# Retention of eight heads beside an MLP on one core: chunk by chunk and placed late, instead of head pair by head pair

## The chip, the cores and the metric

The kernel runs on one core of one Trainium2 chip. The metric is the device time of one execution in microseconds (us), so lower is better. The engines are named as in the profile: PE is TensorE, PEld its weight load, DVE is VectorE, ACT is ScalarE, POOL is GpSimd, and SP is the engine that issues the input loads. "L282" is a line of the kernel that ran. An execution takes about 1.7 us longer than the span of its profile (387.5 against 385.8 for the kernel before).

## The reference

Eight sequences of 576 tokens pass through retention with eight heads of 64. The 4608 token vectors of 512 then pass through an MLP with a hard-swish.

```python
def _attn_ref(q, k, v):                       # each (8, 8, 576, 64)
    scores = np.matmul(q, k.transpose(0, 1, 3, 2)) / np.sqrt(64)
    gamma = 1.0 - 2.0 ** (-5.0 - np.arange(8))
    rel = np.arange(576)[:, None] - np.arange(576)[None, :]
    Dmat = np.where(rel >= 0, gamma[:, None, None] ** rel, 0.0)
    return np.matmul(scores * Dmat, v)

def _moe_ref(x, w_in, w_out):                 # (4608, 512), (512, 2048), (2048, 512)
    h = x @ w_in
    return (h * np.clip(h + 3.0, 0.0, 6.0) / 6.0) @ w_out
```

Because the decay is a power of the distance, retention can be done in chunks of 128 tokens. Inside a chunk it is masked scores times v. Across chunks it is q times a state, which is decayed by `gamma ** 128` a chunk and to which the sum of k times v of the chunk is added. A sequence is four full chunks and a remainder of 64 tokens.

## The kernel before

The kernel takes one **head pair** at a time, over all four full chunks of a batch (a batch is one sequence). `trans` brings k and q to the layout that the scores need, `score` makes scores and states, and `mix` makes the outputs. All PSUM tiles, into which PE's results go, come from one pool of eight, which rotates. [...] marks cuts.

```python
psum = ctx.enter_context(tc.tile_pool(name="psum", bufs=8, space=bass.MemoryType.PSUM))
[...]
def trans(b, pr):
    pst = psum.tile([P, 2 * NCH * P], FP16, tag="pp")
    [... eight transposes: k of chunks 0..3, then q of chunks 0..3 ...]
    t = work.tile([P, 2, NCH, P], FP16, tag="qkt", bufs=3)
    nc.vector.tensor_copy(t[:, 0]..., pst[:, 0:w])        # the k half, on VectorE
    nc.scalar.copy(t[:, 1]..., pst[:, w:2 * w])           # the q half, on ScalarE

def score(b, pr):
    [... scores of two heads into pms[0], pms[1]; k-v products of four chunks into pu ...]
    for h2 in range(2):
        nc.vector.tensor_tensor(out=at, in0=pms[h2], in1=cmask..., op=ALU.mult)
    nc.vector.tensor_copy(ss[:, 0, :], pu[:, 0, :])
    for c in range(1, NCH):                               # the state, chunk after chunk
        nc.vector.scalar_tensor_tensor(
            out=ss[:, c, :], in0=ss[:, c - 1, :], scalar=gch[:, pr:pr + 1],
            in1=pu[:, c, :], op0=ALU.mult, op1=ALU.add)
[...]
def groups(b):
    return [[(trans, 0)],
            [(score, 0), (trans, 1)],
            [(mix, 0), (score, 1), (trans, 2)],
            [(mix, 1), (score, 2), (trans, 3)],
            [(mix, 2), (score, 3), (trans_rem,)],
            [(mix, 3), (score_rem,)],
            [(mix_rem,)]]
```

The MLP runs in nine blocks of 512 tokens. A block has 32 sub-units of four matmuls each: 16 `up` and then 16 `down`. An `up` is followed by a relu on ScalarE and by a multiply on VectorE that needs it. A `down` leaves these two engines nearly free. The groups of the next batch stand at fixed places between sub-units:

```python
def up(kb, fc):
    [... four matmuls into ph ...]
    nc.scalar.activation(u, ph, ACTF.Relu, bias=cb[:, 0:1], scale=1.0 / 6.0)
    nc.vector.scalar_tensor_tensor(out=gts[kb][:, fc, :], in0=u, scalar=1.0,
                                   in1=ph, op0=ALU.min, op1=ALU.mult)
[...]
for g in groups(0):
    run(0, g)                                  # batch 0 wholly ahead of the MLP
for c in range(NCH + 1):
    load(1, c)
    scale(1, c)
for kb in range(NMB):
    gs = groups(kb + 1) if kb + 1 < B else []
    at_sub = {3 + 4 * i: g for i, g in enumerate(gs)}     # sub-units 3, 7, 11, ... 27
    for s in range(NSUB):
        up(kb, s) if s < NFC else down(kb, ...)
        if s in at_sub:
            run(kb + 1, at_sub[s])
        [... every sixth sub-unit: load and scale a chunk of batch kb + 2 ...]
```

`load` brings a chunk of k, q or v (256 KB in rows of 256 bytes). `scale` multiplies it with its decay weights and casts it, on GpSimd. The MLP's weights are fetched by requests in GpSimd's queue.

## Time and profile before

| | before |
|---|---|
| time, median of 4 executions | 386.61 us (386.09 to 387.2) |
| first MLP matmul | 35.58 us |
| first block of the MLP with batch 1 of retention | 58.91 us |
| each of the six next blocks with a batch of retention | 38.60 us |
| each of the two last blocks, no retention | 27.63 us |
| tail after the last block | about 4.2 us |

35.6 + 58.9 + 6 x 38.60 + 2 x 27.63 + 4.2 is the span, to 0.2 us. A block that holds a batch of retention costs 10.97 us more than one that doesn't, and the first block costs another 20.3 us.

First the page of the kernel before: busy time by engine, then the rows of the span in 40 equal slices (each digit is tenths of busy time; PEclk is the granted clock), then the chain of waits.

```profile
PE 331.4 (86%) x2560; PEld 166.9 (43%) x2560; DVE 195.5 (51%) x411; ACT 156.8 (41%) x277; POOL 101.5 (26%) x130
...
PE   0278219899989998999899989998999899999995
...
PEclk9999857999999999999999999999999999999999
DMA  9999999334924492349234923491440001002002
...
PE 65%; DVE 15%; DMA 8%; ACT 4%; issue 3%; POOL 2%; ACTq 0%; SPq 0%; POOLq 0%
```

No engine is full apart from PE. Yet the chain passes through DVE, ACT and DMA for 27% of the span. The PE row shows two places to look at: slices 5 and 6 (from 38.6 us), where PE is almost empty, and the regular "8" in every fourth slice after that.

**The empty stretch.** This is PE's timeline: start in us, length in us, line, operation, operands, count, and in brackets how long PE stood idle before it and what ended that.

```profile
35.58 5.01 PE L282 MATMUL ph<-xt_155,win_153 128*128 128x512 f16 x16
40.43 0.22 PE L153 MATMUL pst<-ident_90,natk_0_463 128*128 128x128 f16 x1
45.57 0.29 PE L153 MATMUL pst<-ident_90,natk_1_475 128*128 128x128 f16 x1 [4.92 <-POOL natk_1_475 L89]
52.84 0.29 PE L153 MATMUL pst<-ident_90,natk_2_487 128*128 128x128 f16 x1 [6.99 <-POOL natk_2_487 L89]
56.19 0.29 PE L153 MATMUL pst<-ident_90,natk_3_499 128*128 128x128 f16 x1 [3.06 <-POOL natk_3_499 L89]
```

After four sub-units (16 matmuls) PE meets the first transposes of batch 1. One group transposes all four chunks, so it waits until the last chunk has been loaded and scaled. PE works through its instructions in order, and the MLP behind it waits too. The loads are late because the weights arrive at the same time. This is the timeline of the queue that issues q, k and v (how long one request of 256 KB occupied the queue):

```profile
9.73 1.25 SPq L61 DMA_DIRECT2D stgk_3_84<-in_k_dram  x1
...
18.66 0.53 SPq L61 DMA_DIRECT2D stgq_0_459<-in_q_dram  x1
...
26.79 6.91 SPq L61 DMA_DIRECT2D stgq_1_471<-in_q_dram  x1
```

A request takes 0.5 to 1.3 us while q, k and v are alone, and 6 to 7 us while the weights come in.

**The regular gaps.** In the up half of a block, VectorE repeats this (its timeline, same columns):

```profile
107.73 2.48 DVE L288 SCALAR_TENSOR_TENSOR gt_1_1048<-u,ph 128x512 f16<-128x512 f32 x4 [1.24 <-ACT u L286]
110.13 0.68 DVE L180 TENSOR_TENSOR at<-pm_1233,cmask 128x512 f16<-128x512 f32 x1
110.73 0.68 DVE L180 TENSOR_TENSOR at<-pm_1234,cmask 128x512 f16<-128x512 f32 x1
111.33 0.28 DVE L187 CAST ss<-pu 128x128 f16<-128x128 f32 x1
111.64 1.11 DVE L189 SCALAR_TENSOR_TENSOR ss<-ss,gch,pu 128x128 f16<-128x128 f16 x3
112.67 0.42 DVE L158 COPY t<-pst 128x512 f16<-128x512 f16 x1
114.33 2.48 DVE L288 SCALAR_TENSOR_TENSOR gt_1_1048<-u,ph 128x512 f16<-128x512 f32 x4 [1.24 <-ACT u L286]
```

And ScalarE does this at the same time:

```profile
113.12 0.58 ACT L160 COPY t<-pst 128x512 f16<-128x512 f16 x1 [3.21 <-DVE t L158]
113.61 2.43 ACT L286 ACTIVATE u<-ph,cb 128x512 f32<-128x512 f32 x4
```

A group takes VectorE 6.60 us (107.73 to 114.33): 5.36 us of work, ending with the copy of the k half, and 1.24 us in which it waits for a relu. ScalarE can't give it that relu sooner: the copy of the q half stands ahead of the relus in its queue, and that copy waits for VectorE's copy of the other half of the same tile. So VectorE's backlog blocks ScalarE, and ScalarE then leaves VectorE idle. PE pays twice in each such group, before transposes and before scores:

```profile
108.47 0.22 PE L153 MATMUL pst<-ident_90,natk_0_551 128*128 128x128 f16 x1 [0.58 <-DVE gt_1_1048 L288]
...
113.76 0.21 PE L170 MATMUL pm_1329<-t 64*128 64x128 f16 x1 [0.45 <-ACT t L160]
```

The tile `pst` is 1024 columns of f16, 2 KiB a partition. The Trainium skill, "PSUM — Partial Sum Buffer", section "PSUM bank collisions raise a hardware error", says that two engines may not read one bank and quadrant at the same time, so that accesses have to be guarded bank by bank; a bank is 2 KiB (its "Specifications"). That fits the trace: all 32 of ScalarE's half copies were released by VectorE's copy, 117.1 us of waiting in all. That the bank is the reason is argued and not tested: the two halves also go into one tile `t`.

### The profile page before, as it was taken

Reading aid. Unit: us, or ns where it says so; the run is one execution under the profiler, and the core shown is the slowest. Engines: PE = TensorE matmul, PEld = TensorE weight load, DVE = VectorE, ACT = ScalarE, POOL = GpSimd, SP = SyncE. Lnnn points to the kernel's source line nnn. Section 1 sums busy time; section 2 is a strip of 40 time slices with the busy share of each in tenths; the row PEclk is TensorE's granted clock in tenths of the full one; section 3 lists DMA queues with packets and bytes.
Section 4 is the critical chain, followed back from the end, with each engine's and each line's share of the span. In section 5 each row is a group of like instructions: output and inputs, shape, how many; then the busy total and the mean of one; then the engine's idle time right before and its main releaser. Section 6 shows DMA issues by size and latency. Waiting matters only on the chain.

```text
span 385.8 us, 6566 instructions
## 1 busy us (share of the span) xinstructions
PE 331.4 (86%) x2560; PEld 166.9 (43%) x2560; DVE 195.5 (51%) x411; ACT 156.8 (41%) x277; POOL 101.5 (26%) x130
## 2 busy tenths in 40 slices
PE   0278219899989998999899989998999899999995
PEld 0154004444544454445444544454445444444442
DVE  3574205760876087608760876087608760731720
ACT  3023203633563356335633563356335633733721
POOL 3761166304520352045203520452030000000000
PEclk9999857999999999999999999999999999999999
DMA  9999999334924492349234923491440001002002
GB/s 179 189 183 196 200 210 202 61 91 127 227 37 96 119 229 37 86 128 224 45 92 121 228 39 82 130 230 39 94 118 23 3 27 61 23 29 82 0 30 81
DMA packets 122303, 42.37 MB, mean 110 GB/s; under 512 B 113568, under 2 KB 117664, under 8 KB 122272
## 3 DMA queue, kind: packets, MB, share of 16 engines
q1 hardware_dynamic: 118080, 37.76, 46.1%
q0 software_dynamic: 4192, 4.19, 6.4%
q8 instruction: 20, 0.33, 0.3%
q14 instruction: 11, 0.09, 0.1%
HBM read 36.70 MB, written 9.44 MB: 120 GB/s over the span
## 4 chain that ended last, share of the span: by engine, by line
PE 65%; DVE 15%; DMA 8%; ACT 4%; issue 3%; POOL 2%; ACTq 0%; SPq 0%; POOLq 0%
PE ph L282 30%; PE pout L298 27%; DMA stgq_1_471<-in_q_dram 6%; DVE at L180 3%; DVE ss L189 3%; ACT u L286 3%; PE pst L153 2%; ACT t L160 2%; DVE gt_6_3688 L288 1%; DMA stgq_3_86<-in_q_dram 1%; DVE gt_3_2104 L288 1%; DMA stgq_3_495<-in_q_dram 1%; PE po L201 1%; PE pu L175 1%; DVE t L158 1%
## 5 line engine op out<-in xcount | busy, mean ns | idle before, releaser
L282 PE MATMUL ph<-xt_155,win_153 128*128 128x512 f16 x576 | 133.0, 387 | 0.0
L286 ACT ACTIVATE u<-ph,cb 128x512 f32<-128x512 f32 x144 | 92.5, 692 | 15.6 <-PE ph L282 15.6
L282 PEld LDWEIGHTS <-win_153 128*128 128x128 f16 x576 | 56.6, 99 | 66.5 <-issue 4.9
L160 ACT COPY t<-pst 128x512 f16<-128x512 f16 x32 | 18.7, 585 | 117.1 <-DVE t L158 117.1
L303 ACT COPY osb<-pout 128x512 f32<-128x512 f32 x36 | 21.1, 586 | 86.9 <-PE pout L298 65.2
L189 DVE SCALAR_TENSOR_TENSOR ss<-ss,gch,pu 128x128 f16<-128x128 f16 x96 | 33.4, 348 | 3.4
L158 DVE COPY t<-pst 128x512 f16<-128x512 f16 x32 | 13.4, 418 | 16.1 <-PE pst L153 16.1
L211 ACT ACTIVATE xt_155<-po 128x512 f16<-128x512 f32 x32 | 19.6, 613 | 1.3 <-PE po L209 0.9
L288 DVE SCALAR_TENSOR_TENSOR gt_8_4362<-u,ph 128x512 f16<-128x512 f32 x16 | 11.0, 688 | 16.6 <-ACT u L286 16.6
L288 DVE SCALAR_TENSOR_TENSOR gt_2_1576<-u,ph 128x512 f16<-128x512 f32 x16 | 10.2, 684 | 12.9 <-ACT u L286 12.9
L288 DVE SCALAR_TENSOR_TENSOR gt_1_1048<-u,ph 128x512 f16<-128x512 f32 x16 | 10.2, 684 | 12.9 <-ACT u L286 12.9
L288 DVE SCALAR_TENSOR_TENSOR gt_3_2104<-u,ph 128x512 f16<-128x512 f32 x16 | 10.2, 684 | 12.9 <-ACT u L286 12.9
L288 DVE SCALAR_TENSOR_TENSOR gt_6_3688<-u,ph 128x512 f16<-128x512 f32 x16 | 10.2, 684 | 12.9 <-ACT u L286 12.9
L288 DVE SCALAR_TENSOR_TENSOR gt_5_3160<-u,ph 128x512 f16<-128x512 f32 x16 | 10.2, 684 | 12.9 <-ACT u L286 12.9
L288 DVE SCALAR_TENSOR_TENSOR gt_4_2632<-u,ph 128x512 f16<-128x512 f32 x16 | 10.2, 684 | 12.9 <-ACT u L286 12.9
L288 DVE SCALAR_TENSOR_TENSOR gt_7_4153<-u,ph 128x512 f16<-128x512 f32 x16 | 11.0, 688 | 11.3 <-ACT u L286 11.3
L170 PEld LDWEIGHTS <-t 64*128 64x128 f16 x256 | 9.5, 97 | 15.4 <-issue 8.5
L288 DVE SCALAR_TENSOR_TENSOR gt_0_520<-u,ph 128x512 f16<-128x512 f32 x16 | 10.5, 685 | 10.9 <-ACT u L286 10.9
L298 PE MATMUL pout<-wout_154,gt_0_520 128*128 128x512 f16 x64 | 14.5, 379 | 0.0
L298 PE MATMUL pout<-wout_154,gt_1_1048 128*128 128x512 f16 x64 | 14.5, 379 | 0.0
L298 PE MATMUL pout<-wout_154,gt_2_1576 128*128 128x512 f16 x64 | 14.5, 379 | 0.0
L298 PE MATMUL pout<-wout_154,gt_3_2104 128*128 128x512 f16 x64 | 14.5, 379 | 0.0
(596 smaller groups left out, 552.9 us busy)
## 6 DMA issues: line engine op xcount, KB each, us to landing
out_dram<-osb SPq DMA_DIRECT2D x36, 256.0 KB, 2.2
win_153<-in_moe_w_in_dram POOLq DMA_DIRECT2D x4, 512.0 KB, 11.4
wout_154<-in_moe_w_out_dram POOLq DMA_DIRECT2D x2, 1024.0 KB, 24.4
stgk_0_66<-in_k_dram SPq DMA_DIRECT2D x1, 256.0 KB, 3.2
stgq_0_68<-in_q_dram SPq DMA_DIRECT2D x1, 256.0 KB, 3.9
stgv_0_70<-in_v_dram SPq DMA_DIRECT2D x1, 256.0 KB, 4.5
stgk_1_72<-in_k_dram SPq DMA_DIRECT2D x1, 256.0 KB, 4.8
stgq_1_74<-in_q_dram SPq DMA_DIRECT2D x1, 256.0 KB, 5.1
```

What stands on the lines that cost most here:

```text
L153: nc.tensor.transpose(pst[:, o:o + P], nat[name, b, c][:, P * pr:P * pr + P], ident16)
L158: nc.vector.tensor_copy(t[:, 0].rearrange("p c s -> p (c s)"), pst[:, 0:w])
L160: nc.scalar.copy(t[:, 1].rearrange("p c s -> p (c s)"), pst[:, w:2 * w])
L170: nc.tensor.matmul(pms[h2][:, c, :], t[r, 0, c, :], t[r, 1, c, :], start=True, stop=True)
L180: nc.vector.tensor_tensor(out=at, in0=pms[h2], in1=cmask[:, 2 * pr + h2, :].unsqueeze(1).to_broadcast([P, NCH, P]), op=ALU.mult)
L189: nc.vector.scalar_tensor_tensor(out=ss[:, c, :], in0=ss[:, c - 1, :], scalar=gch[:, pr:pr + 1], in1=pu[:, c, :], op0=ALU.mult, op1=ALU.add)
L211: nc.scalar.mul(xt16[:, pr, b * S:b * S + NCH * P], po.rearrange("p c s -> p (c s)"), inv_sqrt_d)
L282: nc.tensor.matmul(ph, win16[:, dmc, P * fc:P * fc + P], xt16[:, dmc, tok0:tok0 + MBLK], start=(dmc == 0), stop=(dmc == NCC - 1))
L286: nc.scalar.activation(u, ph, ACTF.Relu, bias=cb[:, 0:1], scale=1.0 / 6.0)
L288: nc.vector.scalar_tensor_tensor(out=gts[kb][:, fc, :], in0=u, scalar=1.0, in1=ph, op0=ALU.min, op1=ALU.mult)
L298: nc.tensor.matmul(pout, gts[kb][:, fc, P * mc:P * mc + P], wout16[:, fc, :], start=(fc == 0), stop=(fc == NFC - 1))
L303: nc.scalar.copy(osb, pout)
```

## The change

The intent is to run retention **chunk by chunk over all eight heads** instead of pair by pair over all chunks, as a pipeline whose step `i` does mix of chunk `i-2`, score of chunk `i-1` and transposes of chunk `i`, and to place each step as late between MLP sub-units as the MLP permits. Four things come with it:

- Transposes need one chunk only, so one late load holds up less.
- The state is one 128x512 add a chunk on VectorE. The decay multiply moves to GpSimd, and the copy of chunk 0's state goes to ScalarE. Three dependent 128x128 operations and a cast go away.
- A deadline of each step is worked out backwards from the block that needs its tokens, `LEAD` = 2.0 sub-units ahead of that block, with at least `GAP` = 6.2 sub-units between steps. Steps stand in the up half and in the down half.
- The second MLP block is split into two of 256 tokens. Weight requests are spread between the first steps.

```diff
-    def trans(b, pr):
-        pst = psum.tile([P, 2 * NCH * P], FP16, tag="pp")
+    def trans(b, c):
[... the remainder chunk: one ScalarE copy ...]
+        pst = psum.tile([P, 2, NPR, P], FP16, tag="pp", name="pst")
         for i, name in enumerate(("k", "q")):
-            for c in range(NCH):
+            for pr in range(NPR):
[...]
+        nc.vector.tensor_copy(t[:, 0], pst[:, 0])
+        nc.scalar.copy(t[:, 1], pst[:, 1])
[... score: two masks of 128x512 as before, now over four pairs of one chunk ...]
-        nc.vector.tensor_copy(ss[:, 0, :], pu[:, 0, :])
-        for c in range(1, NCH):
-            nc.vector.scalar_tensor_tensor(
-                out=ss[:, c, :], in0=ss[:, c - 1, :], scalar=gch[:, pr:pr + 1],
-                in1=pu[:, c, :], op0=ALU.mult, op1=ALU.add)
+        if c == 0:
+            nc.scalar.copy(ss, pu)
+        else:
+            nc.vector.tensor_tensor(out=ss, in0=pu, in1=st.pop(("d", b, c)),
+                                    op=ALU.add)
+        st["s", b, c + 1] = ss
+        if c + 1 < NCH:
+            sd = work.tile([P, NPR, P], FP32, tag="stated", bufs=2)
+            nc.gpsimd.tensor_tensor(out=sd, in0=ss, in1=gch, op=ALU.mult)
+            st["d", b, c + 1] = sd
[...]
+    def step(i):
+        stage(mix, i - 2)
+        stage(score, i - 1)
+        stage(trans, i)
+        stage(load, i + 4)
+        stage(scale, i + 1)
[...]
+    blocks = [(0, 512), (512, 256), (768, 256)] \
+        + [(1024 + 512 * i, 512) for i in range(7)]
[... prologue: chunks 0..3 of batch 0, weight requests between the steps ...]
+    LEAD, GAP = 2.0, 6.2
+    for kb, (tok0, n) in enumerate(blocks):
+        b, s = divmod(tok0 + n - 1, S)
+        g = b * (NCH + 1) + s // P
+        due[g + 2] = min(due[g + 2], starts[kb] - LEAD)
+    for i in range(len(due) - 2, -1, -1):
+        due[i] = min(due[i], due[i + 1] - GAP)
+    for w, f, *a in subs:
+        while nxt < len(due) and due[nxt] <= t:
+            step(nxt)
+            nxt += 1
+        f(*a)
+        t += w
```

## The prediction

> **What bounds it now.** The chain of waits gives TensorE (PE) 65%, VectorE (DVE) 15%, DMA 8%. Read from the timeline, the 385.8 us are three stages.
> - Start: the first MLP matmul comes at 35.6 us. Retention of batch 0 runs pair by pair, and PE waits for VectorE and ScalarE between groups.
> - Stall: after four MLP sub-units PE is all but idle from 40.6 to 57 us. The transposes standing there need all four chunks of batch 1. Weights and q/k/v share the queues: a 256 KB load is issued every 1.2 us alone, every 6.1 to 6.9 us while weights come in (SP timeline, 20 to 40 us). The granted clock is 0.50 from 46 to 62 us.
> - Steady: one block and one batch of retention take 38.6 us. The last two blocks, without retention, take 27.6 us each, 0.863 us a sub-unit. Retention thus costs 11.0 us a batch. The PE timeline holds only about 7.7 us of work for it: transposes 0.45, scores 0.32, k-v products 0.24, mix 0.67 us a group, four groups, and about 0.96 us of remainder. Some 3 us are gaps: 0.6 before transposes (PSUM held by VectorE, which has 3 us of retention work a group: two masks at 0.60, four state ops 1.4, one copy 0.35), 0.45 before scores (ScalarE's copy of the same step).
>
> **What the change does.** Removed: three dependent 128x128 state ops (0.35 us each) and a cast (0.28) per group. Added: one 128x512 add on VectorE (estimate 0.6 us, like the mask), one decay multiply on GpSimd (about 1.04 us, like the scaling there), two more cross matmuls per full chunk (0.06 us). Moved: a step is mix(i-2), score(i-1), transpose(i), one per 6.2 sub-units and also between down sub-units, so nothing in a step waits for that step. VectorE per 6.2 up sub-units: 3.75+2.2 = 6.0 us, against PE 5.35+1.75 = 7.1 us. The PSUM gaps should go: retention about 8.0 us a batch.
>
> The start changes less than it looks. The instruction order puts two steps ahead of the first MLP sub-unit, so the transposes of batch 1 chunk 0 stand before it. They need a q load that landed at 30.7 us before; weights are now asked for earlier and split the engines with it, so I estimate 33 to 37 us and the first MLP matmul at about 36.5 us, as late as before. (The Trainium skill, "DMA: Bandwidth & Descriptors", Queues, rings and completion order, says that each DMA engine alternates between the queues with work; the issue intervals above agree.) From there, thirteen sub-units run freely, and chunks are asked for one by one as they land, so the 16 us stall shrinks to 1 or 2 us.
>
> **Sum.** First MLP 36.5 + 288 sub-units x 0.863 = 248.6 + seven batches of retention 55.9 + waits, cold clock and ScalarE in the two 256-token blocks 3 + tail 4.2 = 348 us. So 17 us come from the stall and about 21 us from the gaps (7 x 3).
>
> Predicted 348 us; 80% range 340 to 357. Faster by over 2%: 0.97; within 2%: 0.02; slower: 0.01.
>
> **Right if** the timeline shows the first MLP matmul at 34 to 39 us; no PE idle of over 3 us after it; a block with five steps at about 35.6 us; VectorE busy about 165 us; idle in front of transposes and scores near zero; last two blocks nearer 27.6 us.
>
> **Wrong if** the batch 1 chunk 0 load lands after 42 us (later start), if GpSimd, now with decay multiplies ahead of scaling in its order, delays chunks, if ScalarE's in-order copies (each waits for VectorE's copy of the same tile) refill PSUM, or if the half-size blocks stall. If the loads land before 30 us, it is about 6 us faster.

## The result and the profile after

The changed kernel takes 346.07 us (345.94 to 346.57), against 386.61. A ratio here is the mean time of one kernel's fast runs over the mean of the other's in the same rounds, so it is not quite the ratio of the medians quoted: 0.8953, with a 95% interval of 0.8938 to 0.8969.

| | before | after |
|---|---|---|
| span of the profile | 385.8 us | 344.4 us |
| first MLP matmul | 35.58 us | 33.70 us |
| block of 512 tokens with retention | 38.60 us (seven groups) | 35.52 us (five steps), 33.70 (four) |
| cost of a batch of retention in a block | 10.97 us | 7.89 us |
| last block (no retention), to the end of its last matmul | 27.79 us | 27.79 us |

The same rows of the page, after:

```profile
PE 321.0 (93%) x2624; PEld 170.1 (49%) x2624; DVE 178.6 (52%) x323; ACT 171.5 (50%) x301; POOL 127.2 (37%) x156
...
PE   0476999999999999999999999999999999999994
...
PE 83%; DMA 7%; POOL 5%; issue 2%; DVE 1%; ACT 1%; POOLq 0%; ACTq 0%
```

VectorE's share of the chain fell from 15% to 1%, although VectorE is busy for the same share of the span. The steady part in the windows view (a stretch, its length, and the busy time of each engine in it): first the kernel before, then the one after, from a block with five steps.

```profile
175.31:213.91 38.60, 36.53 (x307) 18.59 (x305) 21.80 (x46) 17.24 (x30) 12.19 (x15) 1.00 0.53 121
```

```profile
175.06:210.58 35.52, 35.52 (x306) 18.29 (x304) 19.43 (x32) 19.22 (x32) 15.19 (x19) 1.00 0.59 131
```

In a period of one block PE was not busy for 2.07 us (38.60 - 36.53); in the changed kernel's it is busy throughout. The gaps cost more than this idle time shows, because a matmul's record runs on past the moment at which the next one could start. From one matmul's start to the next, the four hold-ups of a block take 0.80, 0.80, 0.67 and 0.67 us; the same four places in experiment 4, where nothing waits, take 0.06, 0.06, 0.15 and 0.15. That is 2.5 us a block. PE's timeline where the stall was:

```profile
33.30 0.61 PE L167 MATMUL pst<-ident_90,natq_0_450 128*128 128x128 f16 x4 [0.21 <-POOL natq_0_450 L91]
33.70 12.71 PE L274 MATMUL ph<-xt_155,win_153 128*128 128x512 f16 x52
...
54.93 0.40 PE L167 MATMUL pst<-ident_90,natq_2_658 128*128 128x128 f16 x4 [0.60 <-POOL natq_2_658 L91]
```

Thirteen sub-units (52 matmuls) run before the next step asks for a chunk, and the longest idle time after that is 0.60 us.

Where the 41.4 us of span came from, each kernel taken as first MLP matmul + nine blocks' worth of MLP at 27.63 + seven batches of retention + tail + the rest:

| term, us | before | after | difference |
|---|---|---|---|
| first MLP matmul | 35.6 | 33.7 | -1.9 |
| MLP, 9 x 27.63 | 248.7 | 248.7 | 0 |
| retention of seven batches | 7 x 10.97 = 76.8 | 7 x 7.89 = 55.2 | -21.6 |
| stall and cold clock (what is left) | 20.5 | 2.5 | -18.0 |
| tail | 4.2 | 4.3 | +0.1 |

Of the 20.5 us before, 15.6 are PE's idle times in the empty stretch above. "Cold clock" stands for the slow pace after idle time: 16 of the MLP's 512-column matmuls start about 427 ns before the next one instead of 216, in two stretches, at 36 and from 57.5 us. In the changed kernel 6 do, all at 33.7 to 36 us.

### The profile page after: what moved, and what is told of

The parts are those of the page before. It is cut to its first block, busy times and chain, and to the rows that moved or that the text cites. A ratio compares the mean times of both kernels' runs of the same rounds, so it can differ in the third digit from the quotient of the medians.

```text
span 344.4 us, 6738 instructions
## 1 busy us (share of the span) xinstructions
PE 321.0 (93%) x2624; PEld 170.1 (49%) x2624; DVE 178.6 (52%) x323; ACT 171.5 (50%) x301; POOL 127.2 (37%) x156
## 4 chain that ended last, share of the span: by engine, by line
PE 83%; DMA 7%; POOL 5%; issue 2%; DVE 1%; ACT 1%; POOLq 0%; ACTq 0%
PE pout L291 36%; PE ph L274 32%; DMA stgv_1_415<-in_v_dram 7%; PE pst L167 4%; PE po L234 3%; PE pu L196 3%; PE po L240 2%; POOL sd L217 1%; POOL win_153 L307 1%; PE pst L159 1%; DVE rmask L139 0%; POOL natk_3_268 L91 0%; POOL natk_2_215 L91 0%; DVE natq_0_158 L91 0%; POOL cmask L134 0%
## 5 line engine op out<-in xcount | busy, mean ns | idle before, releaser
L274 PE MATMUL ph<-xt_155,win_153 128*128 128x512 f16 (+1 forms) x640 | 129.4, 360 | 0.0
L278 ACT ACTIVATE u<-ph,cb 128x512 f32<-128x512 f32 (+1 forms) x160 | 99.3, 650 | 19.5 <-PE ph L274 18.7
L274 PEld LDWEIGHTS <-win_153 128*128 128x128 f16 x640 | 62.3, 98 | 60.8 <-issue 1.7
L217 POOL TENSOR_TENSOR sd<-ss,gch 128x512 f32<-128x512 f16 x24 | 27.9, 1163 | 146.4 <-ACT ss L210 89.4
L243 ACT ACTIVATE xt_155<-po 128x512 f16<-128x512 f32 (+1 forms) x40 | 22.3, 557 | 28.8 <-PE po L240 22.6
L280 DVE SCALAR_TENSOR_TENSOR gt_9_4445<-u,ph 128x512 f16<-128x512 f32 x16 | 11.0, 688 | 11.3 <-ACT u L278 11.3
L212 DVE TENSOR_TENSOR ss<-pu,sd 128x512 f16<-128x512 f32 x24 | 16.3, 680 | 0.0
L291 PE MATMUL pout<-wout_154,gt_8_4072 128*128 128x512 f16 x64 | 14.5, 380 | 0.0
L291 PE MATMUL pout<-wout_154,gt_3_1609 128*128 128x512 f16 x64 | 14.5, 379 | 0.0
L291 PE MATMUL pout<-wout_154,gt_0_492 128*128 128x512 f16 x64 | 14.5, 379 | 0.0
L291 PE MATMUL pout<-wout_154,gt_6_3105 128*128 128x512 f16 x64 | 14.5, 379 | 0.0
L291 PE MATMUL pout<-wout_154,gt_7_3562 128*128 128x512 f16 x64 | 14.5, 379 | 0.0
L291 PE MATMUL pout<-wout_154,gt_5_2583 128*128 128x512 f16 x64 | 14.5, 379 | 0.0
L291 PE MATMUL pout<-wout_154,gt_4_2131 128*128 128x512 f16 x64 | 14.5, 379 | 0.0
L291 PE MATMUL pout<-wout_154,gt_9_4445 128*128 128x512 f16 x64 | 14.0, 379 | 0.0
L280 DVE SCALAR_TENSOR_TENSOR gt_4_2131<-u,ph 128x512 f16<-128x512 f32 x16 | 10.9, 688 | 5.7 <-ACT u L278 5.6
L280 DVE SCALAR_TENSOR_TENSOR gt_3_1609<-u,ph 128x512 f16<-128x512 f32 x16 | 10.6, 686 | 6.2 <-ACT u L278 5.8
L280 DVE SCALAR_TENSOR_TENSOR gt_0_492<-u,ph 128x512 f16<-128x512 f32 x16 | 10.8, 687 | 5.7 <-ACT u L278 5.7
L280 DVE SCALAR_TENSOR_TENSOR gt_5_2583<-u,ph 128x512 f16<-128x512 f32 x16 | 10.9, 687 | 5.4 <-ACT u L278 5.2
```

What stands on the lines that cost most here:

```text
L212: nc.vector.tensor_tensor(out=ss, in0=pu, in1=st.pop(("d", b, c)), op=ALU.add)
L217: nc.gpsimd.tensor_tensor(out=sd, in0=ss, in1=gch, op=ALU.mult)
L243: nc.scalar.mul(xt16[:, :, b * S + P * c:b * S + P * c + n], po, inv_sqrt_d)
L274: nc.tensor.matmul(ph[:, 0:n], win16[:, dmc, P * fc:P * fc + P], xt16[:, dmc, tok0:tok0 + n], start=(dmc == 0), stop=(dmc == NCC - 1))
L278: nc.scalar.activation(u[:, 0:n], ph[:, 0:n], ACTF.Relu, bias=cb[:, 0:1], scale=1.0 / 6.0)
L280: nc.vector.scalar_tensor_tensor(out=gts[kb][:, fc, 0:n], in0=u[:, 0:n], scalar=1.0, in1=ph[:, 0:n], op0=ALU.min, op1=ALU.mult)
```

## The experiments

Two theories of the regular gaps were put up.

- **L, a loop through in-order queues**: the gaps arise where groups follow each other densely in the up half, because VectorE's copy, ScalarE's copy, the relus behind it and VectorE's multiplies wait for one another in turn. Wider spacing or breaking one link removes them.
- **V, the amount of work on VectorE**: the state operations are too many; taking them off VectorE is what removed the gaps.

For the start, **S** says that the decay multiplies in GpSimd's queue, ahead of the scaling, hold back the first MLP matmul. The later experiments deal with the stall and with the start.

The texts name a theory by its letter or by what it says. All ratios are against the kernel before. Every result matched the reference except that of the fifth. Its output is wrong, which doesn't matter for the time.

### 1. Changed kernel, state back on VectorE

```diff
-            nc.vector.tensor_tensor(out=ss, in0=pu, in1=st.pop(("d", b, c)), op=ALU.add)
+            for pr in range(NPR):
+                nc.vector.scalar_tensor_tensor(
+                    out=ss[:, pr, :], in0=prev[:, pr, :], scalar=gch[:, pr, 0:1],
+                    in1=pu[:, pr, :], op0=ALU.mult, op1=ALU.add)
-            nc.gpsimd.tensor_tensor(out=sd, in0=ss, in1=gch, op=ALU.mult)
```

> The changed kernel with its placement kept, but the state decay put back on VectorE: four dependent-free multiply-adds of 128x128 per step (about 1.4 us) in place of one add (0.6), nothing on GpSimd. Theory L (a loop: VectorE's in-order work for a step plus its share of the up sub-units plus about 1.24 us in which VectorE waits for ScalarE, against TensorE's own time): per 6.2 up sub-units the loop is 3.85+3.0+1.24 = 8.1 us against 7.1, but only two or three steps in a row meet up sub-units[...], so a steady block with five steps stays at 35.5 to 36.5 us and the total is 344 to 352. Theory V (the relief of VectorE's state work is what removed the gaps): a steady block of 37.5 to 38.6, total 358 to 368. Theory S (the start is set by GpSimd's queue, where decays wait for states): the first MLP matmul comes earlier than 33.7 us, at 29 to 33.

Measured: 354.24 us, ratio 0.9151 (0.9131 to 0.9171). The steady block with five steps took 35.52 us, exactly as in the changed kernel. So the cheaper state is not needed for the gain in the steady part. All of the loss is at the start, in the opposite direction to S: the first MLP matmul came at 41.83 us instead of earlier than 33.70. PE's timeline:

```profile
34.76 0.61 PE L167 MATMUL pst<-ident,natk 128*128 128x128 f16 x4 [5.57 <-POOL natk L91]
41.43 0.61 PE L167 MATMUL pst<-ident,natq 128*128 128x128 f16 x4 [6.07 <-POOL natq L91]
41.83 8.53 PE L274 MATMUL ph<-xt,win 128*128 128x512 f16 x32
```

Without the decays in its queue GpSimd asked for the first weights at 14.83 us, against 19.15 in the changed kernel. The load of q of batch 1, chunk 0 then met the weights: GpSimd idled for it and scaled it at 40.33 us, against 32.20. The decays help by accident, because they delay the weights.

### 2. Changed kernel, steps dense in the up half

```diff
-    LEAD, GAP = 2.0, 6.2
+    LEAD, GAP = 13.0, 4.0
```

> The changed kernel with cheap state work, but its steps every 4 sub-units and early, in the up half of the block before (lead 13, gap 4), as the kernel before had its groups. Theory L: the loop is 2.48+2.2+1.24 = 5.9 us a step against TensorE's 5.2, so a steady block grows by about 2 us to 37 to 38, and batch 1 is wanted earlier, about 5 us of waiting at the start: total 358 to 368. Theory V: steady block unchanged at 35.5, only the start loses: total 348 to 353. Theory P (crowding alone, whatever the work): a steady block of 38 to 38.6, total 368 to 375.

Measured: 352.75 us, ratio 0.9102 (0.9071 to 0.9133). L's range failed, and V's holds it. Blocks took 33.7 to 36.2 us, and most of the loss is again early (waits of 0.88, 1.75 and 0.60 us for chunks that are now asked for sooner). Density alone does not bring the gaps back. The 0.6 us that some steady blocks lose is another wait, three times, for GpSimd's scaling; experiment 3, without decays on GpSimd, has none for GpSimd there:

```profile
129.53 0.40 PE L167 MATMUL pst<-ident,natq 128*128 128x128 f16 x4 [0.46 <-POOL natq L91]
```

### 3. Both of these at once

```diff
-    LEAD, GAP = 2.0, 6.2
+    LEAD, GAP = 13.0, 4.0
[... and the state edit of experiment 1 ...]
```

> Both of these: steps crowded in the up half and the state work on VectorE. Theory L: loop 2.48+3.0+1.24 = 6.7 us a step against 5.2, steady block 38.5 to 40, total 372 to 386. Theory V: steady block as in the first of these, 37.5 to 38.6, total 362 to 372. Theory P: the same as with cheap state work when crowded, within 2 us.

Measured: 354.85 us, ratio 0.9171 (0.9147 to 0.9194); first MLP matmul at 41.85 us, as in experiment 1; blocks from 33.7 to 36.1 us, and the waits view lists no wait of PE between 100 and 320 us. V is refuted by this, and L in the form it had. VectorE's timeline suggests why:

```profile
193.31 0.42 DVE L170 COPY t<-pst 128x512 f16<-128x512 f16 x1
194.97 2.11 DVE L280 SCALAR_TENSOR_TENSOR gt<-u,ph 128x512 f16<-128x512 f32 x3 [1.24 <-ACT u L278]
197.25 0.69 DVE L280 SCALAR_TENSOR_TENSOR gt<-u,ph 128x512 f16<-128x512 f32 x1 [0.17 <-ACT u L278]
```

The loop is there: 1.24 us idle after the k copy, as in the kernel before. But this step was the remainder's, with one mask of 0.42 us and no state, and after it VectorE has caught up (it waits 0.17 us for the next relu, so it has no backlog). Of the five steps of a batch, one scores the remainder and one scores chunk 0, whose state ScalarE copies. Heavy steps therefore don't follow one another for long, and the backlog drains before it reaches PE. The one block of 36.1 us (113.78 to 149.89) agrees with this: only there do three full steps (chunks 0 to 2) follow one another in the up half, and after the third PE waits for 0.13 us before transposes (at 132.65, for VectorE) and, at the next step, for 0.08 us before scores (at 137.63, for ScalarE's copy). These are read from the single records, since the views list only longer idle times. In the kernel before, every head pair's group is alike.

### 4. Kernel before, the split copy joined on ScalarE

```diff
-        nc.vector.tensor_copy(t[:, 0].rearrange("p c s -> p (c s)"), pst[:, 0:w])
-        nc.scalar.copy(t[:, 1].rearrange("p c s -> p (c s)"), pst[:, w:2 * w])
+        nc.scalar.copy(t.rearrange("p i c s -> p (i c s)"), pst)
```

> The kernel before, with one edit: the whole copy of the transposes (q and k) out of PSUM on ScalarE, so that no ScalarE copy waits behind VectorE's half of it. VectorE loses only 0.35 us of 3.0 a group; ScalarE gains about 0.5. Theory L (the handover VectorE copy, then ScalarE copy, then the relu queued behind it costs 1.24 us a group on the critical loop): a group takes 5.2 to 5.6 us in place of 6.6, a steady block 35 to 36.5 in place of 38.6, total 362 to 376. Theory V (VectorE's load alone): a steady block of 37.5 to 38.2, total 379 to 386.

Measured: 366.7 us, ratio 0.9475 (0.9453 to 0.9498). The block fell from 38.60 to 35.74 us, and PE waits for nothing between 100 and 320 us. VectorE's timeline, and ScalarE's copy:

```profile
209.20 2.48 DVE L286 SCALAR_TENSOR_TENSOR gt<-u,ph 128x512 f16<-128x512 f32 x4
...
213.11 1.11 DVE L187 SCALAR_TENSOR_TENSOR ss<-ss,gch,pu 128x128 f16<-128x128 f16 x3
214.14 2.48 DVE L286 SCALAR_TENSOR_TENSOR gt<-u,ph 128x512 f16<-128x512 f32 x4
```

```profile
211.62 1.01 ACT L158 COPY t<-pst 128x1024 f16<-128x1024 f16 x1 [0.51 <-PE pst L153]
```

A group takes 4.94 us instead of 6.60, and the 1.24 us of idle time is gone. The state work is the same as before. ScalarE now waits 0.51 us for PE instead of 3.21 us for VectorE. One call changed returns about half of the whole gain, which shows the loop in the kernel before. The edit also takes the 0.42 us of VectorE's half off that engine; but experiment 5 takes more off it, leaves the split, and gains less.

### 5. Kernel before, the state made cheap (wrong)

```diff
-        nc.vector.tensor_copy(ss[:, 0, :], pu[:, 0, :])
-        for c in range(1, NCH): [... scalar_tensor_tensor ...]
+        nc.vector.tensor_copy(ss, pu)
```

> The kernel before with VectorE's state work per group cut from 1.4 us to one copy of about 0.6 (the running state is left out, so the result is wrong on purpose). The first runs showed that a steady block of the kernel before loses its 3 us to the cycle: four multiplies, two masks, state, VectorE copy (5.4 us), then 1.24 us of waiting for ScalarE's copy and relu, 6.6 us a group. Theory L: the cycle shortens by 0.8 us to 5.8 in the groups that meet up sub-units, block 36 to 36.9, total 369 to 376. Theory H (only the handover counts, VectorE's load does not): block 38.2 or more, total over 383.

Measured: 372.59 us, ratio 0.9635 (0.9611 to 0.966), relative error 0.555 as intended; block 36.58 us. VectorE's work a group falls by 0.74 us from start to start, and its cycle from 6.60 to 5.84 us; the 1.24 us of waiting in it stay. Less work on VectorE narrows the gaps, but less than breaking the loop does (35.74).

### 6. Kernel before, wider spacing

```diff
-        at_sub = {3 + 4 * i: g for i, g in enumerate(gs)}
+        at_sub = {(9 + 9 * i) // 2: g for i, g in enumerate(gs)}
```

> The kernel before with its groups every 4.5 sub-units in place of 4, from sub-unit 4: of the four groups with scores only two, not three, now fall in the up half, and each has half a sub-unit more. Theory L: gaps arise only where one full group follows another within the up half, so they fall to about a third: block 36.3 to 37.3, total 371 to 380, the start unchanged (no TensorE work between 41 and 57 us). Theory O (pair order itself causes the gaps, wherever groups stand): block 38.3 to 38.6, total 384 to 388.

Measured: 371.35 us, ratio 0.9601 (0.9582 to 0.9619); block 36.52 us. Half a sub-unit more between groups, with two groups with scores instead of three in the up half, is worth as much as taking half of the state's work away. The two parts of this edit were not run apart. Experiments 4 to 6 all reach into the same cycle of 6.60 us.

### 7. Kernel before, joined copy and batch 1 placed late

The edit is that of experiment 4, and in the first block the groups start at sub-unit 10 instead of 3:

```diff
-        at_sub = {3 + 4 * i: g for i, g in enumerate(gs)}
+        at_sub = {(3 + 4 * i if kb else 10 + 3 * i): g for i, g in enumerate(gs)}
```

> The kernel before with the whole copy on ScalarE as in the fourth run, and in the first block alone the groups of batch 1 later: from sub-unit 10 every 3 in place of from 3 every 4. If the stall at the start is only that the transposes need all of batch 1 at 57 us while TensorE has other work, it shrinks by the seven sub-units put ahead of it, 6 us: total 358 to 363. If it is set by the weights or the TensorE clock, it does not shrink: 365 to 368.

Measured: 361.11 us, ratio 0.933 (0.9306 to 0.9354), 5.6 us less than experiment 4. Eleven sub-units now run ahead of the stall instead of four. But it still ends at about 57.8 us, because the first group still needs the fourth chunk. Placement alone takes back 5.6 us.

### 8. Changed kernel without the 256-token blocks

```diff
-    blocks = [(0, 512), (512, 256), (768, 256)] \
-        + [(1024 + 512 * i, 512) for i in range(7)]
+    blocks = [(512 * i, 512) for i in range(NMB)]
```

> The changed kernel with nine blocks of 512 tokens in place of the two of 256. Then the second block needs batch 1 up to its fourth chunk, and step 6 stands before sub-unit 6 in place of 13: it meets the q load of batch 1 chunk 1, ready at 45.9 us, at about 40 us. Expected about 6 us of waiting there, total 350 to 354; if the half blocks bring nothing, or cost what they win in small instructions, 344 to 347.

Measured: 353.18 us, ratio 0.9131 (0.9107 to 0.9155); span 351.7 us, 7.3 more than the changed kernel. Only six sub-units stand in front of the next step now, and PE's timeline shows the stall that comes back:

```profile
47.47 0.61 PE L167 MATMUL pst<-ident,natq 128*128 128x128 f16 x4 [5.66 <-POOL natq L91]
```

So 7.3 of the 18.0 us won from the stall belong to the two half blocks, which move deadlines back. The remaining 10.7 belong to chunk order, late placement and the spread weight requests, which were not run apart.

### 9. Changed kernel, first deadline dropped

```diff
-    for kb, (tok0, n) in enumerate(blocks):
+    for kb, (tok0, n) in list(enumerate(blocks))[1:]:
```

with `LEAD, GAP = 2.0, 5.0`, so that the MLP need not wait for the transposes of batch 1.

> The changed kernel without the deadline that its first block sets (its tokens are done before the loop anyway) and with steps every 5 sub-units in place of 6.2: the transposes of the remainder of batch 0 and of batch 1 chunk 0 then stand before sub-units 10 and 15, not ahead of the first. If the first MLP matmul at 33.7 us waited only for them (GpSimd scales them at 30 to 33 us, behind decays and weight requests), it comes at 29 to 30 us and nothing waits again for over 1 us: total 341 to 344. If the weights or the loads bound the first 60 us in any case, the waits come back before later steps: 345 to 347.

Measured: 345.62 us, ratio 0.8936 (0.8906 to 0.8967), not told apart from the changed kernel. The first MLP matmul came at 29.54 us as expected, 4.2 us sooner, but the span fell by only 1.5 us. The range of 345 to 347 holds the total, but the waits that it named did not come back; only one of 0.80 us for the second weight did:

```profile
29.54 11.39 PE L274 MATMUL ph<-xt,win 128*128 128x512 f16 x40 [0.69 <-ACT xt L243]
...
50.77 1.02 PE L291 MATMUL pout<-wout,gt 128*128 128x512 f16 x4 [0.80 <-DMA wout<-in_moe_w_out_dram]
```

The records of the single matmuls tell where most of the other 2.7 us went. About 1.3 us is pace: 11 of the first 13 steps from one start to the next took 426 or 427 ns, against the first 6 in the changed kernel, and then 216 ns in both. About 1.1 us is retention work (of the remainder of batch 0 and of chunk 0 of batch 1) that now stands behind the first MLP matmul instead of before it. The wait of 0.80 us stands against one of 0.60. Why the slow pace lasted longer was not tested.

### 10. The same, with the prologue reordered

The scaling of chunk 0 moves ahead of the masks, each later chunk's scaling moves ahead of the step before it, and the requests for the first weight go one step earlier:

```diff
+    scale(0, 0, on_vector=True)
     gch = const.tile([P, NPR, P], FP32)
[...]
-        scale(0, c, on_vector=True)
-        if c >= NCH - 2:
+        if c + 1 < NCH:
+            scale(0, c + 1, on_vector=True)
+        if c in (1, 2):
[... rmask copies moved behind this loop ...]
```

> The same, and the start in another order: the first chunk scaled before the mask is built, the next chunk scaled before the decay that waits for a state, the first two quarters of the up weights asked for one chunk earlier. Expected: the first MLP matmul at 24 to 26 us, some waits of 1 to 2 us for down weights or batch 1 around 42 to 50 us, total 337 to 341. If the DMA queues bound the start, it is no better than the run before it (within 1 us).

Measured: 341.28 us, ratio 0.8821 (0.8797 to 0.8845); first MLP matmul at 27.71 us, not 24 to 26; the total just misses 337 to 341. PE still waited 3.84 us at 11.03 us for ScalarE's copy of the transposes. The total is 4.3 us below experiment 9's, so the DMA queues alone did not bound the start.

### 11. Changed kernel, heavy steps forced together in the up half

```diff
-    LEAD, GAP = 2.0, 6.2
+    LEAD, GAP = 19.0, 2.0
[... and the state edit of experiment 1 ...]
```

If the loop is a matter of a run of heavy steps, it has to come back here. A rival held chunk order to be immune.

> A stress of the changed kernel: state work on VectorE (3.0 us a full step) and steps every 2 sub-units early in the up half (lead 19, gap 2), so that full steps follow one another there. Theory L: the cycle of a step is 1.2+3.0+1.24 = 5.4 us against TensorE's 3.5, so TensorE waits for VectorE and ScalarE again, 2 to 4 us in a steady block (37.5 to 39.5 us), and the start waits for all of batch 1: total 368 to 390. If going chunk by chunk is immune in itself, no such waits: steady block 35.5 and total 352 to 362.

Measured: 370.01 us (two executions), ratio 0.9555 (0.9529 to 0.9581). Four of the five measured blocks took 36.3 to 39.0 us and one 34.8. The gaps are back, with the same two marks. First VectorE, then PE:

```profile
212.38 1.29 DVE L280 SCALAR_TENSOR_TENSOR gt<-u,ph 128x512 f16<-128x512 f32 x2 [1.24 <-ACT u L278]
```

```profile
211.81 0.40 PE L191 MATMUL pm<-t 64*128 64x128 f16 x8 [1.26 <-ACT t L171]
```

PE waited 12.6 us for ScalarE's copies over the run, in 18 places. Chunk order is not immune. That it escapes because its heavy steps stand apart is the likely reading; this run changed the state work, the spacing and the lead at once, and the same placement with the cheap state was not run.

### 12. Experiment 10 with the joined copy of experiment 4

```diff
-        nc.vector.tensor_copy(t[:, 0], pst[:, 0])
-        nc.scalar.copy(t[:, 1], pst[:, 1])
+        nc.scalar.copy(t, pst)
```

> The changed kernel with the later demand and the reordered start of the last runs, and the whole copy of the transposes on ScalarE. In the steady part it should change nothing (no TensorE wait there to remove). At the start scores no longer wait for ScalarE's half behind VectorE's (5.0 us of such waits in the run before it), so the first MLP matmul should come at 24 to 26.5 us in place of 27.7; the down weights then may be late by 1 to 2 us. Expected 338.5 to 341 us; if the first 50 us are held by the loads in any case, 341 to 342.

Measured: 340.64 us (five executions), ratio 0.8796 (0.8783 to 0.8809). The interval overlaps that of experiment 10, so the joined copy shows no clear gain once the loop is open: the first MLP matmul came at 27.42 us, short of the 24 to 26.5 expected, and the start still waits 8.4 us for GpSimd's scaling (5.8 of them ahead of the first transpose). Of experiment 10's 3.84 us, 1.10 are left, but 2.59 come up in front of the next transposes, for the next chunk's scaling. It beats both kernels: 0.8796 against 0.8953 is 1.8% less than the changed kernel.

## Why the prediction was right, and where a step of it was wrong

The predicted 348 us (340 to 357) was right; the median was 346.07. The terms, as predicted and measured: first MLP matmul 36.5 and 33.70; MLP 248.6 and 248.7; retention 55.9 (8.0 a batch) and 55.2 (7.89); waits, cold clock and the rest 3 and 2.5; tail 4.2 and 4.3. The predicted sum is a span, so about 1.7 us should have been added for the time of an execution. That omission hid 1.7 of the 3.8 us by which the terms together were too long.

**The gaps: right in size, and right in the risk named.** A block of 35.6 was predicted and 35.52 measured. The prediction said that the gaps would go because VectorE has less to do than PE between two steps. Experiment 3 shows that this is not the necessary part: by its expectation VectorE had 2.48 + 3.0 us to do a step against PE's 5.2, and the gaps stayed away, but for 0.6 us in one block. The risk that the prediction named, ScalarE's in-order copies, did come in experiment 11. Experiments 4 and 11 show the loop itself, in each kernel once. That it is the mix of light and heavy steps in chunk order that opens it is read from experiment 3's timeline (its block of 36.1 us above all) and agrees with experiment 11, but no run isolated it: experiment 11 moved the steps closer together than experiment 3 and also changed how many stand in the up half. One point of its list missed: only the last block is without retention now; the one before it took 32.62 us, because late placement moved steps into it.

**One cause named wrongly.** "0.45 before scores (ScalarE's copy of the same step)" is wrong. The copy that released the scores at 113.76 belongs to the transposes at 108.47, one group earlier. VectorE's half of it started only at 112.67. Both gaps are VectorE's backlog, passed on by the order of the copies. Nor was "nothing in a step waits for that step" new: the groups of the kernel before were skewed in the same way.

**The stall: right.** "From there, thirteen sub-units run freely" is the line with 52 matmuls, and "the 16 us stall shrinks to 1 or 2 us" became 0.60 us. Experiment 8 shows that the half blocks carry 7.3 us of it; experiment 7 shows what placement gives to the old order.

**The start: the step that failed.** The prediction said that the weights "are now asked for earlier", so that the q load of batch 1 lands at 33 to 37 us and the first MLP matmul comes at 36.5. They were asked for later. GpSimd's timeline in the changed kernel:

```profile
16.04 1.16 POOL L217 TENSOR_TENSOR sd<-ss,gch 128x512 f32<-128x512 f16 x1 [3.18 <-ACT ss L210]
...
19.15 1.69 POOL L307 DMA_DIRECT2D win_153<-in_moe_w_in_dram  x2
...
25.58 1.18 POOL L217 TENSOR_TENSOR sd<-ss,gch 128x512 f32<-128x512 f16 x1
26.68 3.03 POOL L311 DMA_DIRECT2D wout_154<-in_moe_w_out_dram  x4
...
32.20 1.05 POOL L91 TENSOR_TENSOR natq_0_450<-stgq_0_340,wq 128x512 f16<-128x512 f32 x1
```

The decay stands in GpSimd's queue ahead of the weight requests and waits for a state. The first request went out at 19.15 us (17.92 before). The q load, issued at 18.70 us, landed 4.0 us later, at 22.7; before it took 12.0 us from 18.66. So the load was no longer the limit. GpSimd's own order was: it scaled q only at 32.20, behind decays and weight requests, and the MLP began at 33.70. The prediction had named decays ahead of the scaling as a risk, but not as what sets the start. That 33.70 came within 3 us of 36.5 (and just under its 34 to 39) is therefore luck: the number was near, the wait behind it was another. The prediction had read the order of the instructions and left out when the engine reaches them. The mechanism it used is real: in experiment 1, where the weights are asked for at 14.83 us, the first MLP matmul does come late (41.83). The Trainium skill, "DMA: Bandwidth & Descriptors", section "Queues, rings and completion order", says that a DMA engine takes packets from its queues in turn; a load of 256 KB that lands in 4.0 us ahead of the weights and in 12.0 us among them agrees.

**Smaller sizes.** VectorE was busy for 178.6 us, not 165. Part of the miss is that multiplies which stand apart no longer overlap in the records (the 16 of a block sum to 10.9 us instead of 10.2), and part is the 16 extra ones of the half blocks. The add took 0.68 us on VectorE (0.60 from start to start in most, as estimated), the decay on GpSimd 1.163 us instead of 1.04. The Trainium skill, "GPSIMD Engine Reference", section "Engine selection", puts two-input work on GpSimd at about twice VectorE's time; these two operations of 128x512, which are not the same one, differ by 1.7.

## What to carry to other kernels

Before blaming an engine's load for the gaps on another, look at who releases whom: here two engines at 51% and 41% busy blocked each other through the order of their queues, and joining one copy gave back half of what the restructured kernel did. Work that another engine waits for should not stand in a queue behind a wait for that engine's backlog; where it must, light steps between the heavy ones may help (experiments 3 and 11 agree with it, none isolates it). When a change puts new work into a queue that also issues loads, work out when the engine reaches each request, since a load asked for later may let another one land sooner.

## What the Trainium skill lacked or had wrong

- "Perfetto Trace Analysis", section "Optimizing Scalar/DVE Operations", says that where Scalar or Vector cause bubbles without being full, "breaking up instructions may allow work to be completed sooner". Here the reverse edit helped: one 128x1024 copy of 1.01 us on ScalarE in place of two halves (0.42 on VectorE, 0.58 on ScalarE) took the kernel before to a ratio of 0.9475 (366.7 us). The page doesn't speak of the order between engines that a split of one tile brings.
- "PSUM — Partial Sum Buffer" gives the rule on two engines at one bank, but not what a guarded split costs in time: 1.24 us of idle VectorE a group here, because ScalarE's relus queue behind the guarded copy.
- "DMA: Bandwidth & Descriptors" says that queues take turns by packet, but not how unequal the turns are: a 256 KB request in rows of 256 bytes went from 0.5 to 1.3 us in the issuing queue to 6 to 7 us while f32 weights were being cast to f16 on the other queue.
- "TensorE: Matmul & The Clock Gate", section "Seeing it yourself", warns that clock events in traces have been unreliable. It has no case of a clock record that reads full speed on a cold array, as here: the PEclk row of the kernel before reads 9 in its first slices. Yet transposes at 19 to 20 us start 107 ns apart, the page's cold pace (its Part 1), and at 108.5 us 56 ns apart, its warm one.
